# Five of nine attention tiles of each head pair transposed by the DMA as fp16 halves, instead of by TensorE in fp32

## The chip, the cores and the metric

The kernel runs on one core of a Trainium2 chip. TensorE does matmuls, and transposes as matmuls against an identity; VectorE (DVE), ScalarE (ACT) and GpSimd (POOL) do elementwise work; SyncE (SP) issues most DMAs, in the order in which they stand in its queue. The metric is the device time of one execution in microseconds, lower is better.

## The reference

Attention over 4 batches of 8 heads, 576 tokens, head size 64, with a threshold near the row's maximum; then a gated layer without an activation, and a second layer with one (all fp32):

```python
scores = scale * np.matmul(q, k.transpose(0, 1, 3, 2))
thresh = np.max(scores, axis=-1, keepdims=True) - tau
scores = np.where(scores >= thresh, scores, -1000000000.0)
scores = scores - np.max(scores, axis=-1, keepdims=True)
attn = np.exp(scores)
attn = attn / (np.sum(attn, axis=-1, keepdims=True) + 1e-09)
attn_out = np.matmul(attn, v)                    # (4, 8, 576, 64)
x = attn_out.transpose(0, 2, 1, 3).reshape(2304, 512)
h = (x @ w1) * (x @ w2) @ w3                     # w1, w2: 512x1024, w3: 1024x1024
x2 = h @ w_out                                   # 1024x512
h2 = x2 @ w_in                                   # 512x2048
y = np.where(h2 > 0, h2, np.exp(np.minimum(h2, 0)) - 1) @ w_out2
```

## The kernel before

**Pairs and tiles.** The 32 heads are 16 pairs, p = 0 to 15, and each pair has 9 tiles of 128 query rows (pos 0 to 8; the last holds the remaining 64 rows of both heads). So there are 144 tiles, i = 0 to 143. Pairs 0 to 3 go first, their first four tiles each, then their last five each; from tile 36 on (pair 4) each pair's nine tiles stand together. A pair's output is formed in two groups: n = 0 of the first four tiles (256 columns of queries a head), n = 1 of the last five (320 columns).

**One tile** is a chain: scores S on TensorE into a PSUM tile `s` (L317 for pairs 0 to 3, L329 later); the negated row maximum on DVE (`emit_max`, L338); a one-column threshold on POOL (`emit_tiny`, L342; for pairs 0 to 3 also a one-column bias, `emit_bias`, L346); the exponential on ACT (`emit_exp`, L351 and L353) into `e`; mask and row sum on DVE (`emit_mask`, L359); five transposes of 128 columns on TensorE back into the same `s` (`emit_X`, L370); and a copy on ACT into `pt`, P transposed (`emit_C`, L381 to L386). The ring of `s` has three tiles, and a slot is held from the scores to that copy. `e` has five buffers, `pt` two.

**After a group's tiles** come the reciprocal row sums on DVE (`emit_rr`, L394 and L395), turned on TensorE (L400), kept by ACT (L405), stored to DRAM by SP (`rd`, L412 and L414) and loaded back, spread over the partitions (`rb`, L422 to L428). P times V is ten fp32 matmuls (five blocks of 128 keys, two heads; each fp32 matmul stands as two instructions in the trace, so 20), the two heads writing different halves of the output partitions (`emit_PV`, L438). DVE multiplies by the reciprocals (`emit_xf`, L446), ACT rounds to fp32r (`emit_xh`, L450), and POOL forms the rest (`emit_xl`, L454): `x` is two fp32r halves.

**The gated layer** (`ab`, L475) of batches 0 to 2 runs in between as filler: 96 units of 12 matmuls (3 batches, 2 groups of columns, 8 weight blocks, 2 weights), which need `x` of a batch's four pairs. ACT keeps one factor (L483), DVE multiplies (L490), SP stores (`g_dr`, L494). The unit of weights `w12` is converted on the way (`conv_ops`, L205 to L230). `keep_busy` (L334) puts four matmuls on ones behind the scores of each of the first 18 tiles. The last batch's 32 units, and all that follows (`m` L743, `x` L883, `h` L916, `o` L945), come after the attention and stand in a fixed order.

**The order** of the attention stage is written by a planner (`Plan`): each operation has an engine, an assumed duration, the operations it follows, and a due time (in tiles); per engine, the operation that can start first goes next, the one due earliest where several can. The order so found is the program's order on each engine, and each engine runs its list in order. FA, FB and FC are the due times of the `ab` units (first batch's two column groups; later batches), C0 and CG those of the weight conversions.

Of the kernel before, what the change touches and what calls it, by code (L numbers as in the profile page):

```python
# [141 lines left out]
def attention_moe_moe2(  # L142
# [205 lines left out]
    def emit_exp(i):
# [3 lines left out]
        else:  # L352
            A.activation(et[i], sc[i][:, :, :HS], AF.Exp, bias=st[i][:, 0:1])  # L353
# [9 lines left out]

    def emit_X(i):
# [3 lines left out]
        for c in range(5):  # L368
            k = min(c * P, S - P)
            T.transpose(o[:, c * P:(c + 1) * P], e[:, k:k + P], ident)  # L370

    def emit_C(i):
        p, pos = SEQ[i]
        j, t = ORDER[pos]
        g = (p, int(pos >= 4))
        if g not in pt:
            pt[g] = ptp.tile([P, 5, 2, NW[1]], F32, tag="pt", name=f"pt{p}_{g[1]}")
        x = sc[i].rearrange("p a b -> p (a b)")[:, :5 * P].rearrange("p (c q) -> p c q", c=5)
        if p < NPL:
            c = (pos - 4 * g[1]) * P  # L380
            A.activation(pt[g].rearrange("p c j t -> p c (j t)")[:, :, c:c + P], x, AF.Copy)  # L381
        elif j == 2:
            A.activation(pt[g][:, :, :, 256:320], x.rearrange("p c (j q) -> p c j q", j=2), AF.Copy)
        else:
            c = (t % 2) * P
            A.activation(pt[g][:, :, j, c:c + P], x, AF.Copy)  # L386
# [43 lines left out]
    def emit_PV(p, n, c):  # L430
# [595 lines left out]
```

## Time and profile before

| | us |
|---|---|
| median of 3 runs (1088.04 to 1089.91) | 1089.19 |
| the profiled execution's own time | 1087.62 |
| its span, from first to last instruction | 1085.8 |
| attention stage, to the last batch's first `ab` matmul | 483.84 |
| the rest, to the end of the span | 602.0 |
| PE busy in the span | 1059.0 |
| DVE, ACT, POOL busy in the span | 554.6, 499.8, 346.5 |

The profiled execution lies 1.6 us under the median. An engine's busy time says how long any instruction of it was running; matmuls overlap each other, so a busy TensorE still may have waited a little. The chain of waits (followed back from the last instruction) says which engine's work each moment of the end time stands on. In the views below, `PEld` is TensorE's weight load, and "<-" in a name means "written from".

### The profile page before, as it was taken

What the parts mean: (1) busy time and instruction counts of PE and PEld (TensorE: products, weight loads), DVE (VectorE), ACT (ScalarE), POOL (GpSimd) and SP (SyncE); (2) the same over time, 40 slices, a digit from 0 to 9 for tenths busy, and PEclk for the clock granted to TensorE, in tenths of its full rate; (3) what the DMA queues carried; (4) which work ended last, traced back from release to release, by engine and by line L of the source; (5) the groups of instructions that cost most, each with busy time, mean ns of one, the idle gap of its engine ahead of it and who ended that gap; (6) DMA issues with size and microseconds to landing.
All of it is one profiled execution on the core that took longest, in us unless ns stands there. A gap on an engine that the chain in (4) does not pass through costs nothing.

```text
span 1085.8 us, 16950 instructions
## 1 busy us (share of the span) xinstructions
PE 1059.0 (98%) x6564; PEld 917.8 (85%) x6564; DVE 554.6 (51%) x998; ACT 499.8 (46%) x822; POOL 346.5 (32%) x418
## 2 busy tenths in 40 slices
PE   7989999999999999999999999999999999999998
PEld 4656777967888889889979999989999999999897
DVE  5887776266555555537483655863232333332322
ACT  3777666276556555534352556533232232322322
POOL 2657544234433332103340223232222222222221
PEclk9999999999999999999999999999999999999999
DMA  9233222213222220026634755300000000000000
GB/s 296 91 110 107 91 80 71 90 59 103 80 68 70 83 80 23 31 104 226 216 121 154 242 191 195 117 1 30 1 1 30 1 30 1 1 30 1 30 1 30
DMA packets 36461, 89.05 MB, mean 82 GB/s; under 512 B 4912, under 2 KB 23580, under 8 KB 31772
## 3 DMA queue, kind: packets, MB, share of 16 engines
q1 hardware_dynamic: 32268, 58.31, 16.9%
q10 hardware_dynamic: 4112, 29.66, 7.9%
q8 instruction: 51, 0.84, 0.3%
q14 instruction: 30, 0.25, 0.1%
HBM read 73.73 MB, written 14.23 MB: 81 GB/s over the span
## 4 chain that ended last, share of the span: by engine, by line
PE 90%; DVE 3%; DMA 2%; ACT 2%; issue 2%; SPq 1%; POOL 0%; DVEq 0%; ACTq 0%
PE h L916 18%; PE o L945 18%; PE ab L475 18%; PE x L883 9%; PE pv L438 8%; PE s L370 7%; PE s L329 5%; PE m L743 4%; PE s L317 2%; DVE e L359 1%; DMA rb<-rd 1%; DMA rqk<-in_qk 1%; DVE st L338 1%; DVE rr L394 1%; ACT e L353 0%
## 5 line engine op out<-in xcount | busy, mean ns | idle before, releaser
L475 PE MATMUL ab<-x,W 128*128 128x256 f32 (+1 forms) x1536 | 234.2, 301 | 1.2 <-DVE g L490 1.2
L475 PEld LDWEIGHTS ab<-x,W 128*128 128x128 f32 x1536 | 209.6, 188 | 12.1 <-issue 6.9
L945 PE MATMUL o<-WO,sl 128*128 128x512 f32 x864 | 215.7, 394 | 0.6 <-POOL sl L937 0.6
L916 PE MATMUL h<-sl,W 128*128 128x384 f32 x1152 | 215.7, 337 | 0.0
L916 PEld LDWEIGHTS h<-sl,W 128*128 128x128 f32 x1152 | 202.8, 188 | 8.3
L945 PEld LDWEIGHTS o<-WO,sl 128*128 128x128 f32 x864 | 161.1, 188 | 30.7 <-POOL sl L937 1.1
L937 POOL TENSOR_TENSOR sl<-th,sl 128x384 fp32r<-128x384 f32 x87 | 88.4, 1017 | 266.5 <-ACT sl L932 266.5
L359 DVE SCALAR_TENSOR_TENSOR e<-s,st,e 128x576 f32<-128x576 f32 x144 | 116.0, 813 | 64.1 <-ACT e L353 50.8
L925 DVE TENSOR_SCALAR th<-h 128x384 f32<-128x384 f32 x96 | 53.4, 556 | 182.3 <-PE h L916 182.3
L926 ACT ACTIVATE th<-th 128x384 f32<-128x384 f32 x96 | 50.4, 525 | 194.0 <-DVE th L925 194.0
L338 DVE TENSOR_REDUCE st<-s 128x1 f32<-128x576 f32 x144 | 107.3, 752 | 52.1 <-PE s L329 38.8
L370 PE MATMUL s<-ident,e 128*128 128x128 f32 x720 | 105.4, 279 | 5.9 <-DVE e L359 5.5
L370 PEld LDWEIGHTS s<-ident,e 128*128 128x128 f32 x720 | 80.1, 141 | 32.4 <-DVE e L359 17.9
L883 PE MATMUL x<-sl,M 128*128 128x384 f32 x576 | 100.9, 337 | 0.2 <-DVE sl L195 0.2
L883 PEld LDWEIGHTS x<-sl,M 128*128 128x128 f32 x576 | 99.7, 188 | 1.3 <-DVE sl L195 1.1
L342 POOL TENSOR_SCALAR st<-st,add 128x1 f32<-128x1 f32 x144 | 43.2, 300 | 172.5 <-DVE st L338 171.9
L438 PE MATMUL pv<-pt,vr 128*64 128x256 f32 (+1 forms) x640 | 94.2, 417 | 0.8 <-DVE g L490 0.8
L353 ACT ACTIVATE e<-s,st 128x576 f32<-128x576 f32 x108 | 78.5, 736 | 32.2 <-DVE st L338 31.7
L386 ACT ACTIVATE pt<-s 128x640 f32<-128x640 f32 x96 | 67.2, 702 | 54.3 <-PE s L370 54.1
L932 ACT ACTIVATE sl<-th 128x384 fp32r<-128x384 f32 x96 | 50.4, 525 | 77.7 <-PE o L945 47.9
L329 PE MATMUL s<-qk 128*128 128x288 f32 x480 | 83.8, 302 | 0.7 <-ACT pt L386 0.6
L930 DVE SCALAR_TENSOR_TENSOR th<-th,h 128x384 f32<-128x384 f32 x96 | 53.2, 554 | 58.6 <-ACT th L926 58.5
(76 smaller groups left out, 1047.4 us busy)
## 6 DMA issues: line engine op xcount, KB each, us to landing
rqk<-in_qk SPq DMA_DIRECT2D x24, 576.0 KB
raw_wo<-in_wo ACTq DMA_DIRECT2D x12, 1024.0 KB
th<-g_dr SPq DMA_DIRECT2D x48, 192.0 KB
raw_w<-in_w SPq DMA_DIRECT2D x8, 1024.0 KB
raw_w<-in_w3t ACTq DMA_DIRECT2D x8, 1024.0 KB
raw_win<-in_win ACTq DMA_DIRECT2D x8, 1024.0 KB
vr<-in_v SPq DMA_DIRECT2D x16, 320.0 KB
g_dr<-g SPq DMA_DIRECT2D x16, 320.0 KB
```

What stands on the lines that cost most here:

```text
L329: T.matmul(s[:, n, :HS], q, k[:, c:c + HS], start=(x == 0), stop=(x == len(ops) - 1))
L338: V.tensor_reduce(st[i][:, 0:1], sc[i][:, :, :HS], axis=AX.XY, op=ALU.max, negate=True)
L353: A.activation(et[i], sc[i][:, :, :HS], AF.Exp, bias=st[i][:, 0:1])
L359: V.scalar_tensor_tensor(et[i], sc[i][:, :, :HS], st[i][:, 1:2], et[i], op0=ALU.is_ge, op1=ALU.mult, accum_out=sm[p][:, pos:pos + 1],)
L370: T.transpose(o[:, c * P:(c + 1) * P], e[:, k:k + P], ident)
L386: A.activation(pt[g][:, :, j, c:c + P], x, AF.Copy)
L438: T.matmul(po_[p, n][j * D:(j + 1) * D, :w], vt[p][:, j, c * D:(c + 1) * D], x_, start=(c == 0), stop=(c == 4),)
L475: T.matmul(o[:, :w], wf[:, m, wx, kt, :], x[:, xx, :], start=(kt == 0 and k == 0), stop=(kt == NK - 1 and k == 2),)
L883: T.matmul(o[:, :TB], M[:, f, mx, e * P:(e + 1) * P], gh[j, f][:, gx, :], start=(k == 0), stop=(k == 23),)
L916: T.matmul(o[:, :TB], WI[f][:, wx, kt, :], xh[j, kt][:, xx, :], start=(k == 0), stop=(k == 3 * NK - 1),)
L937: (V if jobs else G).tensor_tensor(x[:, 1, :], thin[2 + f % 2], f32(x[:, 0, :]), op=ALU.subtract)
L945: T.matmul(po[j, t], gg[j, f][:, gx, t * P:(t + 1) * P], WO[f // 2][:, f % 2, wx, :], start=(f == 0 and k == 0), stop=(f == NF2 - 1 and k ...
```

## The change

The first four tiles of each pair, and all of pairs 0 and 2, stay as they are. The last five tiles of pairs 1, 3 and 4 to 15, 70 tiles, take another way from the mask on: ACT copies the masked `e` as fp16 (`emit_H`), POOL subtracts and writes the fp16 rest (`emit_L`, 512 and 64 columns), and SP issues a DMA transpose of the 128x1152 fp16 tile straight into `pt` (`emit_T`; two of 64 rows for a pair's last tile). The exponential's bias then carries a factor 2^14, which needs `emit_bias` on POOL for those tiles of pairs 4 to 15 too. V of those 14 groups is made fp16 halves as well, scaled by its mean (`v_sum` and `prep_v` on ACT, `v_mean` on TensorE, `v_scale` and `prep_vl` on DVE), and P times V of such a group is 28 fp16 matmuls of 320 columns (14 for each head). `emit_xl` moves from POOL to DVE for all 32 groups. `keep_busy` stands behind 9 tiles instead of 18, `e` has four buffers instead of five, the raw weights `w12` one instead of two. The planner's assumed durations and due times change, and transposes have a queue of their own in it ("DT", 2.7 us each and 2.5 more to land). The core of the diff:

```diff
-EB, PTB, VB = 5, 2, 4
-NKB = 18
+EB, HLB, PTB, VB, VHB = 4, 4, 2, 4, 2
+NKB = 9
...
-FA, FB, FC = (24.0, 44.0), (20.0, 36.0), (8.0, 36.0)
+FA, FB, FC = (22.0, 24.0), (46.0, 32.0), (6.0, 36.0)
...
+    def v_sum(p):
...
+        A.activation(v16[p][:, :, 0, :], vraw[p], AF.Abs, accum_out=vam[p])
+
+    def v_mean(p, i):
+        T.matmul(sc[i][:, 1, HS + P:HS + P + 1], spread, vam[p], start=True, stop=True)
...
+    def prep_v(p):
+        A.activation(v16[p][:, :, 0, :], vraw[p], AF.Copy, scale=vst[p][:, 1:2])
+
+    def prep_vl(p):
+        t = v16[p]
+        V.scalar_tensor_tensor(
+            t[:, :, 1, :], vraw[p], vst[p][:, 1:2], t[:, :, 0, :], op0=ALU.mult, op1=ALU.subtract
+        )
...
+    def of_dma(p, n):
+        return n == 1 and (p >= NPL or p % 2 == 1)
+
+    def by_dma(i):
+
+        return SEQ[i][1] >= 4 and of_dma(SEQ[i][0], 1)
...
+    def emit_H(i):
+        hl[i] = hlp.tile([P, 2 * S], F16, tag="hl", name=f"hl{i}")
+        A.activation(hl[i][:, :S], et[i].rearrange("p a b -> p (a b)"), AF.Copy)
+
+    def emit_L(i):
+        e, t = et[i].rearrange("p a b -> p (a b)"), hl[i]
+        G.tensor_tensor(t[:, S + 64:], e[:, :512], t[:, :512], op=ALU.subtract)
+        G.tensor_tensor(t[:, S:S + 64], e[:, 512:], t[:, 512:S], op=ALU.subtract)
...
+    def emit_T(i):
+        p, pos = SEQ[i]
+        if p >= NPL and ORDER[pos][0] == 2:
+            for j in range(2):
+                SP.dma_start_transpose(pt[p, 1][:, :, j, 256:320], hl[i][j * D:j * D + D, :])
+        else:
+            SP.dma_start_transpose(place(i), hl[i])
...
+    PVS = [(c, x, c) for c in range(5) for x in range(2)] + [(5 + c, 0, c) for c in range(4)]
+    PVC = [PVS[:3], PVS[3:6], PVS[6:9], PVS[9:12], PVS[12:]]
...
+        for c, x, vc in PVC[part]:
+            for j in range(2):
+                x_ = q[:, c, j, :w // D if p < NPL else w]
+                T.matmul(
+                    po_[p, n][j * D:(j + 1) * D, :w], v16[p][:, j, x, vc * D:(vc + 1) * D], x_,
+                    start=(c == 0 and x == 0), stop=(c == 8),
+                )
...
-        G.tensor_tensor(x[:, 1, :], xf[p, n][:, :NW[n]], f32(x[:, 0, :]), op=ALU.subtract)
+        V.tensor_tensor(x[:, 1, :], xf[p, n][:, :NW[n]], f32(x[:, 0, :]), op=ALU.subtract)
...
-        bi = op(call(emit_bias, i), [mx], "POOL", 0.15, i - 10) if plain else mx
+        bi = op(call(emit_bias, i), [mx], "POOL", 0.3, i - 10) if plain or by_dma(i) else mx
...
+        if by_dma(i):
+            hi = op(call(emit_H, i), [mk], "ACT", 0.66, i - 1)
+            rh = take("hl", HLB, hi)
+            lo = op(call(emit_L, i), [hi], "POOL", 1.6, i - 1)
+            re += [mk, hi, lo]
+            cs = [op(call(emit_T, i), [lo], "DT", 2.7, i - 1, 2.5)]
+            rh += [lo] + cs
```

**POOL, last five tiles of pair 14 (tiles 130 to 134).** In these names `st` is a tile's one-column statistics and `hl` its two fp16 halves; the number behind the name is the tile, and a last number tells buffers apart. Before:

```order
L454 TENSOR_TENSOR x13_1_4718<-xf13_1_4711,x13_1_4718 128x320
L342 TENSOR_SCALAR st131_4737<-st131_4737,add2_107 128x1
L342 TENSOR_SCALAR st132_4771<-st132_4771,add2_107 128x1
L342 TENSOR_SCALAR st133_4805<-st133_4805,add2_107 128x1
L342 TENSOR_SCALAR st134_4824<-st134_4824,add2_107 128x1
L454 TENSOR_TENSOR x14_0_4866<-xf14_0_4853,x14_0_4866 128x256
L342 TENSOR_SCALAR st135_4883<-st135_4883,add2_107 128x1
```

Now:

```order
L381 TENSOR_SCALAR st131_5074<-st131_5074 128x1
L377 TENSOR_SCALAR st131_5074<-st131_5074,add2_113 128x1
L381 TENSOR_SCALAR st132_5087<-st132_5087 128x1
L377 TENSOR_SCALAR st132_5087<-st132_5087,add2_113 128x1
L405 TENSOR_TENSOR hl131_5153<-e131_5123,hl131_5153 128x512
L406 TENSOR_TENSOR hl131_5153<-e131_5123,hl131_5153 128x64
L381 TENSOR_SCALAR st133_5160<-st133_5160 128x1
L377 TENSOR_SCALAR st133_5160<-st133_5160,add2_113 128x1
L381 TENSOR_SCALAR st134_5166<-st134_5166 128x1
L377 TENSOR_SCALAR st134_5166<-st134_5166,add2_113 128x1
L405 TENSOR_TENSOR hl132_5162<-e132_5133,hl132_5162 128x512
L406 TENSOR_TENSOR hl132_5162<-e132_5133,hl132_5162 128x64
```

Each of these tiles had one short instruction of POOL, and now has four: bias and threshold, which the exponential and the mask wait for, and the two subtractions, which stand in the same queue between those of later tiles. The subtractions of `x` are gone from POOL.

**SP, around the same tiles.** `rd` is the store of the reciprocal row sums of pair 14, groups 0 and 1, and `rb` their load; `g_dr` is a store of the gated layer. Before:

```order
L414 DMA rd14_0_4748<-rt14_0_4743 4x128
L425 DMA rb14_0_4778<-rd14_0_4748 128x1x256
L494 DMA g_dr_67<-g2_1_6_4734 128x2x320
L414 DMA rd14_1_4916<-rt14_1_4911 5x128
L425 DMA rb14_1_4952<-rd14_1_4916 128x1x256
L494 DMA g_dr_67<-g2_0_0_4902 128x2x256
L428 DMA rb14_1_4952<-rd14_1_4916 128x1x64
```

Now:

```order
L474 DMA rd14_0_5084<-rt14_0_5082 4x128
L434 DMA_TRANSPOSE pt14_1_5063<-hl130_5061 128x9x128
L485 DMA rb14_0_5125<-rd14_0_5084 128x1x256
L434 DMA_TRANSPOSE pt14_1_5063<-hl131_5153 128x9x128
L434 DMA_TRANSPOSE pt14_1_5063<-hl132_5162 128x9x128
L571 DMA g_dr_67<-g2_0_0_5142 128x2x256
L434 DMA_TRANSPOSE pt14_1_5063<-hl133_5202 128x9x128
L474 DMA rd14_1_5262<-rt14_1_5254 5x128
L432 DMA_TRANSPOSE pt14_1_5063<-hl134_5222 128x9x64 x2
L485 DMA rb14_1_5301<-rd14_1_5262 128x1x256
L488 DMA rb14_1_5301<-rd14_1_5262 128x1x64
```

Six transposes stand in SP's queue between the first store of pair 14 and the last load; a load of the reciprocals goes out only when the transpose ahead of it has been issued, and that one only when POOL has written its `hl`.

**TensorE, from the scores of tile 63 (pair 7).** `ab` names end in batch (attached), column group, weight block and weight. Before, with the many equal rows of units 0_1_0_1 to 0_1_7_0 left out:

```order
L329 MATMUL s64_2069<-qk10_1080 128x288 x4
L475 MATMUL ab0_0_7_1_2080<-x3_0_753,W7_1180 128x256 x3
L475 MATMUL ab0_1_0_0_2102<-x0_1_910,W0_274 128x320 x3
...
L475 MATMUL ab0_1_7_1_2345<-x2_1_1249,W7_1180 128x320 x3
L475 MATMUL ab0_1_7_1_2345<-x3_1_1415,W7_1180 128x320 x3
L370 MATMUL s62_2045<-ident_108,e62_2084 128x128 x5
L370 MATMUL s63_2064<-ident_108,e63_2094 128x128 x5
L370 MATMUL s64_2069<-ident_108,e64_2108 128x128 x5
```

Now:

```order
L364 MATMUL s64_2313<-qk10_1121 128x288 x4
L552 MATMUL ab0_1_4_1_2323<-x0_1_918,W4_743 128x320 x3
L552 MATMUL ab0_1_4_1_2323<-x1_1_1176,W4_743 128x320 x3
L552 MATMUL ab0_1_4_1_2323<-x2_1_1306,W4_743 128x320 x3
L552 MATMUL ab0_1_4_1_2323<-x3_1_1605,W4_743 128x320 x3
L364 MATMUL s65_2346<-qk11_1259 128x288 x4
L460 MATMUL s64_2313<-ident_114,rr6_1_2343 5x128
L552 MATMUL ab0_1_5_0_2357<-x0_1_918,W5_1022 128x320 x3
L552 MATMUL ab0_1_5_0_2357<-x1_1_1176,W5_1022 128x320 x3
L552 MATMUL ab0_1_5_0_2357<-x2_1_1306,W5_1022 128x320 x3
L442 MATMUL s63_2300<-ident_114,e63_2353 128x128 x4
```

Before, the second column group of the first batch, 16 units, stood as one run between the scores of tile 64 and the transposes of tiles 62 to 64, behind the last unit of the first group; now such units stand singly between tiles. Up to the scores of tile 36, 5.5 units of `ab` stand in TensorE's list before and 10.25 now; up to those of tile 72, 32 and 31. The P times V of the last five tiles of pairs 8 to 14 stands behind the scores of the fifth tile of the next pair, before and now; that of pairs 3 to 5 stood behind the third or fourth, and now behind the sixth or seventh.

## Rows read from the trace of the kernel before

**Rows 1.** The page: TensorE's busy time and instructions; its granted clock in 40 slices.

```profile
PE 1059.0 (98%) x6564; PEld 917.8 (85%) x6564; DVE 554.6 (51%) x998; ACT 499.8 (46%) x822; POOL 346.5 (32%) x418
...
PEclk9999999999999999999999999999999999999999
```

**Rows 2.** Chain of waits, its longest pieces in order of time: start, length, what.

```profile
63.56 6.89 DMA rb<-rd
...
189.59 29.58 PE ab L475 x204
...
470.85 4.26 PE ab L475 x36
475.11 2.84 PE pv L438 x20
...
483.84 51.15 PE ab L475 x384
```

**Rows 3.** Chain of waits, shares by line, in 0:119, 119:190, 119:484 and 264:484.

```profile
by line: PE s L317 20.6%; PE s L370 13.7%; PE pv L438 12.5%; DMA rqk<-in_qk 9.3%; PE ab L475 5.9%; DMA rb<-rd 5.8%; issue 5.3%; SPq L259 3.9%; DVE e L359 3.5%; PE k L334 3.3%; DVE rr L394 3.3%; ACT pt L381 2.8%; DVE st L338 1.5%; ACT e L351
...
by line: PE pv L438 23.4%; PE s L329 22.5%; PE s L370 16.0%; PE ab L475 9.8%; DVE e L359 9.2%; issue 4.6%; DVE st L338 4.1%; DVE rr L394 3.6%; ACT e L353 1.9%; PE s L400 1.7%; ACT qk L279 1.6%; DVE g L490 0.8%; ACT x L450 0.4%; DVE rr L395 
...
by line: PE ab L475 36.5%; PE pv L438 18.3%; PE s L329 16.1%; PE s L370 16.1%; DVE e L359 2.7%; issue 2.3%; ACT e L353 1.5%; DVE st L338 1.4%; DMA rb<-rd 1.2%; PE s L400 0.9%; DVE rr L394 0.7%; ACT qk L279 0.6%; ACT pt L386 0.6%; DVE g L490
...
by line: PE ab L475 44.1%; PE pv L438 18.8%; PE s L370 17.3%; PE s L329 16.2%; DVE e L359 0.8%; PE s L400 0.7%; DVE st L338 0.7%; ACT e L353 0.6%; DVE g L490 0.4%; issue 0.3%; ACT rt L405 0.2%; DVEq L490 0.0%; DVEq L359 0.0%
```

**Rows 4.** Stretches: length; busy (instructions) of PE, PEld, DVE, ACT, POOL; clock, DMA, GB/s.

```profile
119.00:190.00 71.00, 67.98 (x509) 53.45 (x508) 49.91 (x107) 47.99 (x77) 30.46 (x51) 1.00 0.26 81
190.00:219.00 29.00, 29.00 (x201) 29.00 (x200) 7.07 (x18) 6.85 (x14) 7.95 (x10) 1.00 0.25 84
264.00:484.00 220.00, 218.70 (x1638) 187.51 (x1637) 119.81 (x259) 116.75 (x195) 65.18 (x108) 1.00 0.21 64
119.00:484.00 365.00, 356.51 (x2638) 300.73 (x2637) 207.26 (x448) 202.70 (x335) 123.09 (x197) 1.00 0.23 70
```

**Rows 5.** Groups by form, DVE, 119:190: shapes, count; busy us, mean ns; idle before.

```profile
L359 DVE SCALAR_TENSOR_TENSOR e<-s,st,e 128x576 f32<-128x576 f32 x27 | 21.4, 810 | 1.1 <-ACT e L353 0.7
...
L394 DVE TENSOR_SCALAR rr<-sm 128x5 f32<-128x5 f32 x3 | 2.8, 923 | 0.0
```

**Rows 6.** Groups by form, TensorE, 264:484.

```profile
L370 PE MATMUL s<-ident,e 128*128 128x128 f32 x310 | 45.4, 277 | 0.1
```

**Rows 7.** Timeline of TensorE, 290:297: start, length, line, operation, shapes, count.

```profile
291.18 1.92 PE L475 MATMUL ab<-x,W 128*128 128x320 f32 x12
292.93 0.70 PE L329 MATMUL s<-qk 128*128 128x288 f32 x4
```

**Rows 8.** Groups by form, the whole span.

```profile
L386 ACT ACTIVATE pt<-s 128x640 f32<-128x640 f32 x96 | 67.2, 702 | 54.3 <-PE s L370 54.1
...
L334 PE MATMUL k<-spread 128*128 128x128 f32 x72 | 10.5, 290 | 0.0
...
L342 POOL TENSOR_SCALAR st<-st,add 128x1 f32<-128x1 f32 x144 | 43.2, 300 | 172.5 <-DVE st L338 171.9
...
L230 POOL TENSOR_TENSOR W<-w_win,W 128x1024 fp32r<-128x1024 f32 x8 | 19.3, 2418 | 69.4 <-ACT W L227 69.4
...
L454 POOL TENSOR_TENSOR x<-xf,x 128x320 fp32r<-128x320 f32 x16 | 14.0, 876 | 39.5 <-ACT x L450 39.5
...
L454 POOL TENSOR_TENSOR x<-xf,x 128x256 fp32r<-128x256 f32 x16 | 11.8, 736 | 17.6 <-ACT x L450 17.1
...
L446 DVE TENSOR_TENSOR xf<-pv,rb 128x320 f32<-128x320 f32 x16 | 7.8, 489 | 5.8 <-DMA rb<-rd 2.3 <-PE pv L438 1.7 <-PE s L370 1.5
```

**Rows 9.** The line of DVE's reciprocal sums: count, min/median/max ns, first and last start.

```profile
L394 DVE TENSOR_SCALAR rr<-sm x32: 161/191/1972, 23.1 to 467.6; 128x4 f32<-128x4 f32 x16, 128x5 f32<-128x5 f32 x16
```

**Rows 10.** The DMA queue's own waits: engine, line, what for; total, times, longest.

```profile
SPq L425 <- DMA rd<-rt: 26.6, 23, 2.8
```

**Rows 11.** The page, DMA queue of SP: packets, MB, share of 16 engines' span.

```profile
q1 hardware_dynamic: 32268, 58.31, 16.9%
```

More of the change, by code (lines that the diff above doesn't have):

```diff
@@ L368, in emit_X @@
         for c in range(5):
-            k = min(c * P, S - P)
-            T.transpose(o[:, c * P:(c + 1) * P], e[:, k:k + P], ident)
+            k = min(P, S - c * P)
+            T.transpose(o[:k, c * P:(c + 1) * P], e[:, c * P:c * P + k], ident)
     def emit_C(i):
[L373 to L386, printed above, removed]
+        x = sc[i].rearrange("p a b -> p (a b)")[:, :5 * P].rearrange("p (c q) -> p c q", q=P)
+        A.activation(place(i), x, AF.Copy)
     rrs, rts, rdr, rbc, po_, xf, xT = {}, {}, {}, {}, {}, {}, {}
@@ L496, in store_g @@
         )
-    V.memset(spread, 1.0)
+    V.memset(spread, 1.0 / VSCALE)
     for p in range(NPL):
@@ L567, in attention_moe_moe2 @@
     for p in range(NPAIR):
-        lv = op(call(load_v, p), (), "SP", 0.1, AT[p, 0] - 3, 4.0)
-        VV[p] = [lv]
-        ring["v", p] = take("vr", VB, lv)
+        t0 = AT[p, 0]
+        lv = op(call(load_v, p), (), "SP", 0.1, t0 - 6, 4.0)
+        rv = ring["vr", p] = take("vr", VB, lv)
+        VV[p, 0] = VV[p, 1] = [lv]
+        if not of_dma(p, 1):
+            continue
+        t0 = AT[p, 4] - 1
+        vm = op(call(v_sum, p), [lv], "ACT", 0.8, t0 - 3)
+        am = take("am", 2, vm)
+        i = t0 + 3
+        vs = op(call(v_mean, p, i), [vm, S_[i]], "PE", 0.15, t0 - 1)
+        am.append(vs)
+        ve = op(call(v_scale, p, i), [vs], "DVE", 0.3, t0 - 1)
+        ring["s", i] += [vs, ve]
+        rt = take("vst", 5, ve)
+        vh = op(call(prep_v, p), [ve], "ACT", 0.8, t0)
+        vl = op(call(prep_vl, p), [vh], "DVE", 1.17, t0)
+        rv += [vm, vh, vl]
+        rt += [vh, vl]
+        ring["vst", p] = rt
+        ring["v16", p] = take("v16", VHB, vm)
+        VV[p, 1] = [vh, vl]
     for p in range(NPL, NPAIR):
@@ L620, in attention_moe_moe2 @@
         rb.append(xo)
-        ring["v", p].append(pv)
+        if of_dma(p, n):
+            ring["vst", p].append(xo)
+            ring["v16", p].append(pv)
+        else:
+            ring["vr", p].append(pv)
         ring["pt", p, n].append(pv)
         xh = op(call(emit_xh, p, n), [xo], "ACT", (0.36, 0.42)[n], q)
-        xl = op(call(emit_xl, p, n), [xh], "POOL", (0.73, 0.91)[n], q)
+        xl = op(call(emit_xl, p, n), [xh], "DVE", (0.4, 0.46)[n], q)
         rx += [xh, xl]
```

110 lines of the change are left out of this document (77 added, 33 removed).

## The prediction

> **What bounds the kernel now.** I read the page first: TensorE is busy for 1059 us of the span of 1085.8, in 6564 matmuls, and its granted clock stands at 9 or more tenths in every slice [rows 1]. Such a row does not say that matmuls set the end at every moment, so the chain of waits comes next. From 483.84 us on it is the last batch's `ab` and then the later layers, which the change does not touch [rows 2]; those 602 us I leave as they are. In front of that lie three stretches. From 0 to 119 us (36 tiles, pairs 0 to 3) TensorE's lines make only 56% of the chain (20.6, 13.7, 12.5, 5.9, 3.3), so some 52 us there are waits. From 119 to 190 they make 73.4%, and from 264 to 484 they make 97.1%; over the whole of 119 to 484 they make 87.9% of 365 us, that is 321 us of matmuls and 44 us of waits [rows 3]. In between, at 189.6 us, stands one run of 29.58 us of `ab` alone [rows 2], in which DVE and ACT are busy for 7 of 29 us [rows 4]. Over 119 to 484 DVE is busy for 207 us, ACT for 203 and POOL for 123 [rows 4]. So from 119 us on TensorE's amount of work is the bound, and before that the tile chain.
>
> **What the change removes from TensorE.** In the stretch from 264 to 484 the transposes hold 17.3% of 220 us [rows 3], and there are 310 of them, 62 tiles' worth [rows 6]: 0.614 us a tile. Pairs 4 to 15 lose 60 of these groups: 36.8 us. Over the longer stretch the same division gives 16.1% of 365 for 109 tiles, 0.54 us, which is the lower bound (32 us).
>
> P times V of a last-five group takes 2.84 us now [rows 2]. The new one has 14 pairs of fp16 matmuls of 320 columns. A unit of 12 single-pass matmuls of 320 columns starts at 291.18 and the next work at 292.93 [rows 7]: 0.146 us each. That the two heads' matmuls run side by side, in different output partitions, is seen from the fp32 ones: 20 instructions in 2.84 us are 0.142 us for 320 columns, 0.44 ns a column, while fp32 matmuls on the full width need 10.5 us for 72 of 128 columns [rows 8], 1.14 ns a column. So I take 14 x 0.146 = 2.05 us, and gain 0.79 x 12 = 9.5 us. Were the fp16 pairs to run one after another, a group would take 28 x 0.146 = 4.09 us, 1.25 more than today; the sum would be 24.5 us worse. Nothing in the trace shows an fp16 matmul; I take the pair, since the nearest row, the fp32 one, has it.
>
> `v_mean` adds 12 matmuls of one column. Their bound is the 0.146 us of a full-width fp32 instruction: +1.8 us.
>
> The units of `ab` that now stand before tile 36 (10.25 instead of 5.5) take 4.75 x 1.42 us (36 matmuls in 4.26 us, [rows 2]) = 6.7 us out of the later stretch and put them among the 52 us of waits of the first one. The run of 29.58 us is dissolved by the same move; this changes no amount of TensorE's work, but the other engines work beside it.
>
> In the first stretch 10 transposing groups (6.1 us), two P times V (1.6 us) and nine `keep_busy` (36 x 0.146 = 5.3 us) go and 6.7 us come. I count that stretch at nothing, since the chain there waits for 52 us anyway; its bounds are 6 us either way. The cover of the removed `keep_busy` is the granted clock, which stays up now [rows 1]; if it fell to 1.2 GHz in the waits of that stretch, its 67 us of matmuls would partly double, so this price could reach 10 us.
>
> TensorE's work from 119 to 484 becomes 321 - 36.8 - 9.5 + 1.8 - 6.7 = 270 us.
>
> **What it adds elsewhere.** ACT: the fp16 copy (576 columns) stands in for a copy of 640 at 0.702 us [rows 8], I take them as equal; the two passes over V at that same price are 12 x 1.4 = 17 us on an engine with 160 us free. POOL: by the rows of 256 and 1024 columns (0.736 and 2.418 us [rows 8]) a column costs 2.2 ns, and 512 plus 64 columns come to 1.6 us a tile; 60 tiles are 97 us, 60 biases at the 0.300 us of the threshold [rows 8] are 18, and the moved `x` rests save 12 x 1.61 = 19. POOL goes from 123 to 219 us. That is for fp32; with an fp16 operand it may be half or double, and double would be 316 us. DVE: 24 `x` rests at about 0.49 us [rows 8], 12 of `prep_vl` at about 0.9 and the small `v_scale`: 12 x 2.2 = 26 us, so 207 becomes 233. All stay under TensorE's 270.
>
> A DMA transpose moves 128 x 1152 fp16, 0.29 MB. No row shows one. The lower bound is its bytes: SP's queue moved 58.31 MB in 16.9% of the span [rows 11], 0.318 MB a us, so 0.93 us. The upper is the longest `rb` load on the chain, 6.89 us [rows 2]. A store of the row sums holds back the load behind it for 26.6/23 = 1.2 us [rows 10], so I take some 2.5 us. It matters only above a limit: five transposes a pair, at a pair's 27 us, may take 5.4 us each. The landing is covered too: P times V of pairs 8 to 14 still stands behind the scores of the next pair's fifth tile, five tiles or about 15 us on, and of those the mask (0.81 us [rows 5]), two passes of its like for maximum and exponential, the fp16 copy and the rest take about 3 x 0.81 + 0.70 + 1.6 = 4.7 us. In the list of SP the loads of the reciprocals now stand behind transposes, which wait for POOL; a late `rb` holds `emit_xf`, and behind it all of DVE.
>
> One wait grows for certain. The reciprocal sums on DVE, 0.161 us at the shortest, took up to 1.972 [rows 9], and 0.923 in the mean of three where POOL works long [rows 5]. The longer ones start under a long POOL instruction. The 36 new two-input operations of DVE and 24 such sums will meet POOL at work 219 of some 320 us: 0.67 x half of 1.3 us is 0.44 us each for the 36, and a third of a POOL instruction's half more for the sums, 16 + 5 = 21 us of DVE. DVE has slack, so I put 10 on the path.
>
> The Trainium skill ("SBUF — State Buffer", section "Who interferes with whom") says that a DVE instruction with two inputs in SBUF, or a tensor_scalar in a fast mode, and a GpSimd instruction that reads SBUF exclude each other for the whole instruction. The trace agrees in the reciprocal sums, 0.161 against 1.972 us; for the two-input form it would give the 21 us above, and without it only the 5 us of the sums.
>
> **The sum.** 270 us of matmuls, the 44 us of waits, 10 more: 324 for 365, a gain of 41. The profiled execution's 1087.6 become 1046.2, and with the 1.6 us by which the median lies above it 1048; I say 1047. The pace this asks of the tile chain, 324/109 = 2.97 us a tile, is slower than what it ran at from 119 to 190, 71/27 = 2.63 us a tile [rows 4, 5], with three score tiles then held until the copy; the 70 tiles now free theirs after the mask.
>
> **The rivals.**
> *More is gained.* The waits shrink with the work: at the share of today, 12.1%, 270 us give 307 in all, and with 6 us of the first stretch the time is 1025. For it speaks the freed score ring; against it that DVE's slack falls.
> *Part is eaten.* The fp16 pairs run in turn (24.5 us), or DVE's 21 us and late `rb` loads all count: 1060 to 1085.
> *Slower: the chain, not TensorE.* The share of waits of 119 to 190, 26.6% [rows 3], over all the new work: 270/0.734 = 368 for 365; with DVE's 21 us in full 389, and 1113. It decides from a share of 26%. POOL at double price ends there too. For it: DVE's share rises to that of that stretch (50 of 71 us [rows 4]). Against it: that stretch had little `ab` to fill in, 15 - 5.5 units for three pairs, where now each pair has some seven.
> *Slower: the transposes are the bound.* 70 of them from about 75 us on, with 25 us behind the last: 75 + 70 t + 25 against 484, so from t = 5.5 us. At 6.89 us it is 582, and the time 1187. For it: nothing known of t. Against it: bytes alone need 0.93.
> The Trainium skill ("VectorE: DVE Perf Modes", "The three transpose paths") has 1309 ns for one 128x128 block through the DMA; nine in turn would be 11.8 us, and the estimate from that 1528 us. Another page ("Advanced Engine Details and Errata", "X-Bar Transpose (TRN2)") has transposes as fast as other DMAs, which is the lower bound. No row shows either; the first alone I give 2 in 100, within the chance of this rival.
>
> **How the numbers follow.** The forecast (1030 to 1062) gets 0.60, more gained 0.14, part eaten 0.13, no change 0.02, the chain 0.06, the transposes 0.05. The three runs before lie within 0.2%, which is about what a measurement can tell here; so faster 0.87, same 0.02, slower 0.11. The range runs from 1022 (just under the case of more gained) to 1085 (all of part eaten), and leaves out the slower cases and a little below.
>
> **What would show it.** Right: the last batch's `ab` starts near 442 us instead of 483.84; 74 groups of transposes at about 0.61 us; the new P times V near 2.05 us; TensorE over 80% of the chain from tile 36 on; no long run of `ab`. Wrong: matmuls of P times V that wait for a DMA, a P times V near 4 us, POOL's subtractions well over 1.6 us, DVE's two-input operations far over 0.5 us, a granted clock below full in the first 60 us. The forecast fails most surely if transposes take over 5.5 us each, or if the waits pass a quarter of the attention stage.

## The result, and the profile after

| | before | after |
|---|---|---|
| median us (4 runs each) | 1088.65 | 1072.68 (1071.12 to 1075.20) |
| ratio, 95% interval | | 0.9854 [0.9832, 0.9876] |
| profiled execution | 1087.62 | 1072.06 |
| span | 1085.8 | 1070.3 |
| last batch's `ab` starts | 483.84 | 468.14 |
| the rest, to the end | 602.0 | 602.2 |

Faster by 1.5%, 16 us where 41 were forecast. The whole of it lies in the attention stage: the last batch's `ab` starts 15.7 us earlier, and what follows takes as long as before. The page after, to be read against [rows 1] and [rows 11] (busy time, share and instructions; then tenths of the clock in 40 slices; then the DMA queue's packets, MB and share of 16 engines):

```profile
PE 1016.3 (95%) x6318; PEld 888.7 (83%) x6318; DVE 584.4 (55%) x1072; ACT 515.0 (48%) x864; POOL 440.1 (41%) x586
...
PEclk9999999998999999999999999999999999999999
...
q1 hardware_dynamic: 115532, 78.97, 30.1%
```

TensorE lost 43 us of busy time, POOL gained 94 and VectorE 30, and SP's queue holds the DMA engines for 322 us (30.1% of 1070.3) where it held them for 183. The end of the attention stage, from the chain of waits (start, length, what), against [rows 2]:

```profile
447.32 5.07 DMA rb<-rd
459.48 4.41 DMA pt<-hl
463.93 3.58 PE pv L510 x27
468.14 51.15 PE ab L552 x384
```

Before, `ab` and P times V stood on that path back to back; now a load of reciprocals, a transpose and a P times V at the slower clock come just ahead of the last run (granted clock 0.50 from 464 to 466 us). The trace follows this chain back only to 379.6 us; of the 88 us from there to the last `ab`, TensorE's lines hold 49%, where over 80% was named as a sign of being right:

```profile
by line: PE ab L552 19.5%; PE pv L510 11.4%; DMA pt<-hl 8.2%; PE s L364 7.9%; PE s L442 7.5%; DVE e L394 6.4%; DMA rb<-rd 5.8%; issue 4.1%; POOL hl L405 4.0%; DVE st L373 3.1%; PE pv L502 2.8%; DVE x L531 2.7%; DVE rr L454 2.6%; DMA rd<-rt
```

Where the time came from is seen best in stretches that end at the same tile, the scores of tile 36 (first instruction of that line: 118.8 before, 129.0 after) and those of tile 90 (290.7 and 290.5). Busy time by engine, clock and DMA share, before:

```profile
0.00:119.00 119.00, 105.68 (x761) 68.37 (x762) 86.45 (x164) 76.22 (x108) 65.52 (x107) 0.99 0.45 144
...
290.00:483.84 193.84, 192.54 (x1449) 165.23 (x1447) 104.94 (x227) 101.69 (x171) 56.68 (x94) 1.00 0.20 61
sum 483.84, PE 462.03 PEld 368.94 DVE 293.71 ACT 278.92 POOL 188.61; mean PE 115.51 PEld 92.23 DVE 73.43 ACT 69.73 POOL 47.15
```

and after:

```profile
0.00:129.00 129.00, 108.74 (x748) 68.93 (x749) 88.47 (x175) 79.84 (x118) 66.99 (x113) 0.95 0.55 151
129.00:257.00 128.00, 108.77 (x821) 92.84 (x819) 96.79 (x208) 87.26 (x148) 94.52 (x155) 0.97 0.74 138
257.00:290.00 33.00, 33.00 (x246) 29.60 (x246) 19.81 (x44) 19.71 (x35) 17.91 (x29) 1.00 0.58 136
290.00:468.14 178.14, 168.97 (x1343) 148.43 (x1341) 118.76 (x259) 106.67 (x187) 102.29 (x176) 0.99 0.52 122
sum 468.14, PE 419.47 PEld 339.80 DVE 323.83 ACT 293.50 POOL 281.71; mean PE 104.87 PEld 84.95 DVE 80.96 ACT 73.37 POOL 70.43
```

In the sums, TensorE is busy 42.6 us less (462.03 to 419.47), but idle 48.7 us where it was idle 21.8. The difference, 15.7 us, is the gain. By tile 90, with 40 of the 70 tiles done the new way, nothing was gained. By the starts of the row maxima, 13 us were lost up to tile 36 (133, before 120), 22 won back by tile 72 (227, before 236), where the lone run of `ab` stood, and 9 lost again by tile 81 (258 both). The 30 tiles after tile 90 gave 16.

Who made VectorE wait from tile 36 on (us in total, times, longest), before:

```profile
DVE e L359 <- ACT e L353: 50.8, 46, 1.9
DVE g L490 <- PE ab L475: 49.4, 25, 5.4
DVE st L338 <- PE s L329: 38.8, 41, 2.6
DVE xf L446 <- DMA rb<-rd: 5.4, 3, 2.8
```

and after:

```profile
DVE e L394 <- ACT e L388: 24.5, 27, 1.9
DVE xf L521 <- PE pv L510: 13.0, 4, 6.1
DVE g L567 <- PE ab L552: 12.1, 10, 3.0
DVE xf L521 <- DMA rb<-rd: 10.6, 5, 3.1
DVE e L394 <- POOL st L377: 7.7, 11, 1.7
DVE xf L519 <- DMA rb<-rd: 6.9, 5, 2.5
DVE st L373 <- PE s L364: 6.8, 10, 1.6
```

Before, VectorE waited for TensorE's scores and `ab`, 88 us of them: TensorE was the bound. Now that is 19 us. The largest wait, for ScalarE's exponentials, is half of what it was (24.5 of 50.8), and new waits are for DMA loads (17.5), for POOL, and for P times V, whose own wait was for the DMA (the page's group of L510 has 10.0 us idle, 7.8 of it for `pt`).

One such place, from the timeline (start, length, engine, line, operation, idle before):

```profile
229.28 2.09 PE L510 MATMUL pv<-pt,v 128*64 128x320 f16 x28
...
245.39 3.98 SPq L432 DMA_TRANSPOSE pt<-hl  x2
...
251.10 0.30 PE L510 MATMUL pv<-pt,v 128*64 128x320 f16 x1 [2.44 <-DMA pt<-hl]
251.60 3.59 PE L510 MATMUL pv<-pt,v 128*64 128x320 f16 x27 [0.20 <-DMA pt<-hl]
255.23 0.55 DVE L521 SCALAR_TENSOR_TENSOR xf<-pv,vst,rb 128x320 f32<-128x320 f32 x1 [3.97 <-PE pv L510]
```

The ninth tile of a pair is transposed in two halves, the last thing ahead of P times V. SP issues them from 245.39 to 249.37; TensorE waits for them 2.44 us, its clock falls (granted 0.50 from 252 to 255 us; an earlier fall, from 242 to 245, was over by then), so the same 28 matmuls that took 2.09 us at 229 take 3.9, and VectorE, with every mask behind `xf` in its list, waits 3.97.

### The profile page after: what moved, and what is told of

Its sections match the earlier page's. It is cut to its first block, busy times and chain, and to the rows that moved or that the text cites. A ratio compares the mean times of both kernels' runs of the same rounds, so it can differ in the third digit from the quotient of the medians.

```text
span 1070.3 us, 17023 instructions
## 1 busy us (share of the span) xinstructions
PE 1016.3 (95%) x6318; PEld 888.7 (83%) x6318; DVE 584.4 (55%) x1072; ACT 515.0 (48%) x864; POOL 440.1 (41%) x586
## 3 DMA queue, kind: packets, MB, share of 16 engines
q1 hardware_dynamic: 115532, 78.97, 30.1%
## 4 chain that ended last, share of the span: by engine, by line
PE 59%; DMA 2%; DVE 2%; POOL 1%; ACT 1%; issue 1%; SPq 0%; POOLq 0%; DVEq 0%; ACTq 0%
PE h L1031 19%; PE o L1060 19%; PE x L998 9%; PE ab L552 6%; PE m L858 4%; PE pv L510 1%; DMA pt<-hl 1%; PE s L364 1%; PE s L442 1%; DVE e L394 1%; DMA rb<-rd 0%; DMA th<-g_dr 0%; POOL hl L405 0%; DVE st L373 0%; PE pv L502 0%
## 5 line engine op out<-in xcount | busy, mean ns | idle before, releaser
L394 DVE SCALAR_TENSOR_TENSOR e<-s,st,e 128x576 f32<-128x576 f32 x144 | 115.3, 813 | 40.0 <-ACT e L388 24.5
L405 POOL TENSOR_TENSOR hl<-e,hl 128x512 f16<-128x512 f32 x70 | 82.7, 1181 | 32.8 <-ACT hl L401 32.4
L364 PEld LDWEIGHTS s<-qk 128*128 128x128 f32 x480 | 69.1, 190 | 16.9 <-issue 6.4
L446 ACT ACTIVATE pt<-s 128x640 f32<-128x640 f32 x74 | 51.6, 702 | 41.0 <-PE s L442 36.8
L442 PE MATMUL s<-ident,e 128*128 128x128 f32 (+1 forms) x370 | 56.0, 285 | 9.1 <-DVE e L394 9.0
L235 POOL TENSOR_TENSOR WO<-w_wo,WO 128x1024 fp32r<-128x1024 f32 x12 | 29.9, 2488 | 79.7 <-ACT WO L232 77.3
```

What stands on the lines that cost most here:

```text
L364: T.matmul(s[:, n, :HS], q, k[:, c:c + HS], start=(x == 0), stop=(x == len(ops) - 1))
L394: V.scalar_tensor_tensor(et[i], sc[i][:, :, :HS], st[i][:, 1:2], et[i], op0=ALU.is_ge, op1=ALU.mult, accum_out=sm[p][:, pos:pos + 1],)
L405: G.tensor_tensor(t[:, S + 64:], e[:, :512], t[:, :512], op=ALU.subtract)
L442: T.transpose(o[:k, c * P:(c + 1) * P], e[:, c * P:c * P + k], ident)
```

## The experiments

Four theories of the missing 25 us. **A**: POOL's list (biases, thresholds and subtractions in one queue) holds the tile's chain. **B**: the DMA brings P and the reciprocals late. **C**: VectorE's own load. **D**: the clock, since `keep_busy` went. Beside these, the order and the buffers. "Tile 36" is the start of its row maximum on VectorE, the 37th of that group (120 us before, 133 after). Such a time is of one profiled execution; in e2, which edits only the tiles from 36 on, it is 138, so a few us there tell little. Where no other kernel is named, the edit is to the changed kernel (1072.68 us). Where an operation changes its engine or a ring its size, the planner's entry for it changes too. Ratios are to the kernel before.

**e1, plain copies.**

```diff
-SP.dma_start_transpose(place(i), hl[i])
+SP.dma_start(place(i), hl[i].rearrange("p (c t) -> p c t", c=TPP))
```

> The changed kernel, but each DMA transpose is a plain DMA copy of the same bytes to the same place (P then reaches P times V untransposed: this part of the computation is left out). The accounts so far: against the kernel before, 36 us of the attention stage were to be gained from tile 36 on and 10 us were lost ahead of it; TensorE stands idle 48 us before the last batch's ab, where it stood 22. Theory A (POOL's queue: biases, thresholds and subtractions in one list hold the tile's chain): nothing changes, 1070 to 1075 us. Theory B (the DMA engines, 0.80 busy from 129 to 202 us, bring P and the reciprocals late): 1056 to 1065 us, with the PE waits for pt and DVE waits for rb gone, if the copies are lighter for the DMA engines than the transposes; if the DMA share of 129 to 202 us stays near 0.8, this run says nothing of B.

Measured 1065.29 us, 0.9789 [0.9741, 0.9837]: 7.4 less, its interval just touching that of the changed kernel. From 129 to 202 us the last-but-one column, the DMA share, is 0.80 in the changed kernel

```profile
129.00:202.00 73.00, 65.30 (x513) 56.22 (x513) 58.11 (x124) 51.61 (x89) 55.50 (x92) 1.00 0.80 141
```

and here

```profile
129.00:202.00 73.00, 68.22 (x536) 58.82 (x535) 59.69 (x126) 54.54 (x93) 59.05 (x95) 1.00 0.59 149
```

so the copies are lighter, and SP issues one in 0.63 us (median) instead of 1.31. VectorE's waits for `rb` from tile 36 on fall from 17.5 us to 8.8. B has a part, at the small end of its range; whether by the DMA engines' load or by SP's time to issue isn't told apart.

**e2, no bias on POOL from tile 36 on.**

```diff
-bi = op(call(emit_bias, i), [mx], "POOL", 0.3, i - 10) if plain or by_dma(i) else mx
+bi = op(call(emit_bias, i), [mx], "POOL", 0.3, i - 10) if plain else mx
```

> The changed kernel without POOL's bias for the tiles from 36 on (P is not scaled by 2^14 there, so its fp16 halves keep fewer bits; 60 POOL instructions of 0.2 to 0.3 us go, and the exponential waits for the maximum alone). Theory A: ACT waited some 25 us for biases in all, 8.5 us of it from tile 36 on, and the maximum-to-exponential hop gets about 0.4 us shorter per tile; 1062 to 1069 us. Theory B (DMA) and theory C (VectorE's own load): 1070 to 1075 us.

Measured 1067.69 us, 0.9793 [0.9775, 0.9811]: 5.0 less, as A said.

**e3, the subtraction on VectorE** (`G.` becomes `V.` in `emit_L`).

> The changed kernel with the subtraction that makes P's low fp16 half on VectorE instead of POOL (512 and 64 columns, an estimated 0.8 us a tile there, from the 0.54 us of a two-input subtraction of 320 columns with POOL at rest, instead of 1.56 us on POOL). POOL falls by some 109 us, VectorE rises by some 55. Theory A (POOL's list): 1060 to 1069 us. Theory C (VectorE is the fuller engine up to tile 81, 58 of 73 us from 129 to 202, and everything that it gets more is late): 1077 to 1095 us. Theory B: near 1072.

Measured 1099.38 us, 1.0088 [1.0072, 1.0104]: 26.7 more. The two pieces take 0.68 and 0.22 us there (medians):

```profile
L405 DVE TENSOR_TENSOR hl<-e,hl x70: 673/683/1935, 87.1 to 479.9; 128x512 f16<-128x512 f32 x70
L406 DVE TENSOR_TENSOR hl<-e,hl x70: 208/218/1446, 87.7 to 480.5; 128x64 f16<-128x64 f32 x70
```

VectorE's busy time rises by 57 us (641.4 from 584.4), POOL's falls by 97, and nearly half of VectorE's rise is on the path. So VectorE has little slack (C), and the subtraction stands rightly on POOL.

**e4, 18 `keep_busy` again** (`NKB = 18`).

> The changed kernel with the 18 keep_busy groups of before instead of 9. Theory D (the clock: the granted clock is 0.87 to 0.96 in the slices from 40 to 120 us, where it stood at 1.00): the mean clock rises from 0.989 to at least 0.994 and the time falls to 1065 to 1069 us. Theories A, B and C: 36 more matmuls of 0.13 us in a stretch that waits, 1071 to 1076 us.

Measured 1075.03 us, 0.9862 [0.9832, 0.9893], mean clock 0.981: no gain, and D's remedy doesn't hold the clock.

**e5, pairs 1 and 3 back on TensorE.**

```diff
-return n == 1 and (p >= NPL or p % 2 == 1)
+return n == 1 and p >= NPL
```

> The changed kernel, but the last five tiles of pairs 1 and 3 (10 of the first 36 tiles) stay fp32 on TensorE as before; all later pairs go through the DMA. The first 36 tiles took 10 to 14 us longer after the change. If the new steps of a tile (fp16 copy, subtraction, transpose, the two passes over V) make that, tile 36 comes at 120 to 124 us instead of 130 to 133 and the time is 1062 to 1067 us. If the order does (the units of ab ahead, one buffer instead of two for the loads of w12, the place of the first loads), tile 36 stays near 131 us and the time is 1071 to 1077 us.

Measured 1073.28 us, 0.9852 [0.9825, 0.9879]; tile 36 at 132 us. The new steps don't make the lateness of the first 36 tiles, and ten removed tiles there gain nothing.

**e6, the due times of before** (FA, FB, FC).

> The changed kernel with the due times of ab of before (24 over 44, 20 over 36, 8 over 36). If the units of ab that were drawn ahead of tile 36 make its lateness, tile 36 comes at 120 to 125 us; what of it stays at the last batch's ab depends on whether the run of ab alone comes back near tile 63 to 72: 1064 to 1070 us if it doesn't, 1072 to 1080 if it does. If the new steps make it, tile 36 stays near 131 us and the time is 1072 to 1085 us.

Measured 1090.59 us, 0.9998 [0.9972, 1.0024], above both ranges; tile 36 at 133 us. Without the new due times the change gains nothing. The chain of waits shows why:

```profile
162.59 20.07 PE ab L552 x138
```

The run of `ab` alone is back, at tile 45 to 63, and in 160 to 180 us VectorE works 7.0 us of 20 and ScalarE 5.2. Tile 63 comes 23 us later than in the changed kernel (228, 205), and the last batch's `ab` 19 us later (487.4, 468.1): the rest has no slack in which to catch up.

**e7, the rest of `x` on POOL** (`V.` becomes `G.` in `emit_xl`).

> The changed kernel with the rest of x (32 subtractions of 256 or 320 columns) back on POOL. VectorE loses 32 x 0.55 to 0.82, some 21 us, POOL gets an estimated 26 us. e3 gave VectorE 40 us of busy time more up to 468 us and the time rose by 27 us. Theory C (VectorE's share of the chain sets the pace): two thirds of 21 us, so 1056 to 1066 us. Theory A (POOL's list): 1074 to 1082 us. If both count: near 1070.

Measured 1070.07 us, 0.9838 [0.9798, 0.9878]: not told from the changed kernel. Neither C's two thirds of 21 us nor A's loss shows; the time is where both together were expected, so the two may cancel.

**e8, the reciprocals' stores and loads from ScalarE** (`SP.` becomes `A.` in `store_r` and `load_r`).

> The changed kernel with the stores and loads of the reciprocals (rd, rb) issued by ScalarE instead of SP, so that they stand behind no transpose in SP's list. After the change SP waited 3.3 us a time for the store of rd where it waited 1.2 us, and VectorE's xf waited 10.6 us for rb. Theory B in the form that SP's list holds rb back: 1062 to 1068 us. If it is the DMA engines' own load (0.80 busy from 129 to 202 us), or POOL or VectorE: 1071 to 1080 us, the more since ScalarE pays some 0.5 us an issue (76 issues).

Measured 1069.45 us, 0.9818 [0.9792, 0.9843]: 3.2 less by the medians, between the two ranges, the intervals overlap. That the reciprocals stand behind transposes in SP's list is at most a small part.

**e9, the kernel before with one buffer for `w12`.**

```diff
-name=f"raw_{key[0]}{key[1]}", bufs=2)
+name=f"raw_{key[0]}{key[1]}", bufs=1 if key[0] == "w12" else 2)
```

> The kernel before, with one buffer instead of two for the loads of w12, and nothing else of the change. In e4 to e6 tile 36's maximum came at 132 to 137 us (120 before) whether or not the first pairs went through the DMA and whichever due times stood. If the single buffer makes that, tile 36 comes at 127 to 133 us here and the time is 1092 to 1102 us. If not, tile 36 stays at 119 to 122 us and the time at 1087 to 1091 us.

Measured 1094.50 us, 1.0047 [1.0027, 1.0066], tile 36 at 127 us. One line of the change, which the prediction passed over, costs 5 us.

**e10, the kernel before with the new due times.**

> The kernel before, with the new due times of ab (22 over 24, 46 over 32, 6 over 36) and nothing else of the change. e6 was as slow as the kernel before without them. If the new order carries the gain by itself: 1068 to 1076 us. If it only lets the removed work count (TensorE of before was idle for 8 us from tile 36 on, so that an order can give no more there): 1080 to 1092 us.

Measured 1086.83 us, 0.9968 [0.9955, 0.9980]. Tile 36 comes at 130 us here too; the 10 us are won back by tile 72 (235, before 236). The new order draws work ahead, and gives about 3 us alone.

**e11, e2 + e7 + e8 together.**

> The changed kernel with e2, e7 and e8 together: no bias on POOL from tile 36 on (P unscaled there, so its fp16 halves keep fewer bits), the rest of x on POOL, the reciprocals on ScalarE's queue. If the three waits are different ones, their gains of 5.0, 2.6 and 3.2 us add: 1059 to 1064 us. If they are one wait seen from three sides (the chain of a tile), 1065 to 1069 us.

Measured 1065.42 us, 0.9774 [0.9732, 0.9816]: 7.3 less by the medians. The interval, some 1060 to 1070 us, holds the 10.8 of the sum too, so three waits and one wait seen from three sides are not told apart.

**e12, only pairs 8 to 15 by the DMA.**

> The changed kernel, but only pairs 8 to 15 (from tile 72 on, 40 of the 70 tiles) go through the DMA; the 30 others stay fp32 on TensorE. If a removed transpose and the cheaper P times V pay wherever they stand, 0.61 + 0.16 us a tile come back 30 times: 1085 to 1097 us. If they pay only where TensorE is the bound, and the tile chain sets the pace ahead of tile 72: 1066 to 1076 us.

Measured 1078.61 us, 0.9901 [0.9870, 0.9933]: 5.9 us for 30 tiles put back by the medians, 0.2 a tile (the intervals just touch). Neither range: early tiles pay about a quarter of the 0.77 us that a tile takes off TensorE.

**e13 and e14, smaller rings, with two and one buffers for `w12`.** Both have `EB` 3 for 4 and `HLB` 2 for 4; e13 also the two buffers of before.

> The changed kernel with two buffers for the loads of w12 again; to make room, 3 buffers instead of 4 for P and 2 instead of 4 for its fp16 halves. Compared with e14, which has the same small rings and one buffer. If the single buffer holds back the first 36 tiles here as it did in e9: tile 36 comes 5 to 9 us earlier than in e14 and the time is 4 to 7 us lower. If the loss there has another cause: within 2 us of e14.

> The control of e13: the changed kernel with 3 buffers instead of 4 for P and 2 instead of 4 for its fp16 halves, and one buffer for w12 as in the changed kernel. If the steps of a tile (copy, subtraction, transpose) hold a buffer no longer than some three tiles, nothing changes: 1070 to 1076 us. If the rings themselves hold the chain: 1078 to 1095 us.

e14 measured 1099.96 us, 1.0096 [1.0060, 1.0132], e13 1088.27 us, 0.9988 [0.9975, 1.0002]. The small rings cost 27 us, the second buffer is worth 12 beside them. But tile 36 comes at 132 and 133 us, and the two part from there to tile 45 (159 and 169): so the single buffer was a cost here too, and not the cause of the first 36 tiles' lateness.

**e15, e11 with the plain copies of e1.**

> e11 (three reliefs) with the plain DMA copies of e1 in place of the transposes (P reaches P times V untransposed: this part of the computation is left out). If the DMA's load is a cost apart from POOL and VectorE, the gains add, 1065.4 - 7.4: 1055 to 1060 us. If the copies only shortened the same chain: 1062 to 1067 us.

Measured 1054.40 us, 0.9687 [0.9656, 0.9718]: 11.0 under e11, the intervals clear of each other. What the transposes cost against copies (B) is apart from the part of POOL and VectorE, and together they are 18 us.

**e16, whole-tile transposes twice.**

```diff
-SP.dma_start_transpose(place(i), hl[i])
+for _ in range(2):
+    SP.dma_start_transpose(place(i), hl[i])
```

> The changed kernel with every whole-tile DMA transpose (58 of the 82 instructions) issued twice to the same place, so that SP issues 58 x 1.3 us more and the DMA engines carry some 2 us a tile more (141 us of 16 engines for 70 tiles now, by the queue's share). If the transposes are hidden behind a tile's pace of 2.7 us: 1071 to 1077 us. If the DMA's load sets the pace ahead of tile 81 (0.80 busy from 129 to 202 us): 1085 to 1110 us.

Measured 1234.23 us, 1.1347 [1.1308, 1.1386], far above both ranges. The edit did more than double a load. Both transposes write the same place, and SP issued the second only when the first had landed, as SP's own waits (whole span) say:

```profile
SPq L435 <- DMA pt<-hl: 156.5, 58, 6.3
```

SP stands still for 156.5 us, 2.7 us a time, and the kernel is 161.5 us slower. All else in SP's list stands behind these waits. The other engines' waits from 129 to 560 us:

```profile
PE pv L511 <- DMA pt<-hl: 56.1, 14, 14.5
...
DVE xf L522 <- DMA rb<-rd: 46.6, 5, 14.1
...
POOL rqk L271 <- DMA rqk<-in_qk: 98.6, 11, 17.8
```

P, the reciprocals and the next pair's Q and K all come late, though the DMA engines are busy for only 0.62 to 0.67 of 129 to 428 us. So this run can't tell what the transposes' load costs: the time that it lost is about that of the waits in SP's list. From tile 36 to 143 it takes 453 us (154 to 607) for 107 tiles, 38 us a pair, in which nine whole transposes pass (four twice, the ninth tile once): 4.2 us each, these waits included, is an upper bound. How fast transposes pass without them wasn't measured.

**e17, e11 with the fifth buffer of P back** (`EB` 5; 7 for 8 of the first `x` ring, one for two turned reciprocals).

> e11 (three reliefs) with 5 buffers for P again instead of 4; to make room, 7 instead of 8 for x of the first four tiles and one instead of two for the turned reciprocals. If the rings still hold the chain at 4 (e14, with 3 and 2, was 27 us slower than with 4 and 4): 1056 to 1062 us. If four are enough: 1063 to 1070 us, as e11's 1065.4.

Measured 1072.08 us, 0.9853 [0.9823, 0.9883], above both ranges and 6.7 more than e11. The buffers it borrowed cost more than the fifth of P gives.

**e18, the kernel before with one buffer for `w12` and four for P.**

> The kernel before with one buffer instead of two for w12 and 4 instead of 5 for P: the room that the change takes, and nothing else of it. e9 measured the first of these at 1094.5 us, 4.8 above before. If the fifth buffer of P is spare in the kernel before, where P waits for TensorE's transposes alone: 1092 to 1097 us. If it isn't: 1098 to 1110 us.

Measured 1096.57 us, 1.0066 [1.0053, 1.0079]: the room that the change takes costs 7 us here, some 5 of it the `w12` buffer by e9; the intervals of the two runs overlap, so the fifth buffer of P is not shown to cost anything.

## Why the prediction was right and wrong

**The work that goes from TensorE was right.** I went through TensorE's instructions ahead of the last `ab` and counted each from its start, or the end of the one before it, to its end, by line. Transposes: 91.3 to 49.4 us for 350 fewer, 0.60 us a tile (0.614 forecast). P times V: 88.2 to 80.5, 0.55 a group against 0.79; at full clock a new group takes the 2.09 us shown above, against 2.05 forecast, so the heads' fp16 matmuls do run side by side. `keep_busy`: -4.6. `v_mean`: +2.0 (1.8 forecast). Together 52 us; by the forecast's prices the whole stage was to lose 58.

**Ten of them came back as slower matmuls.** Scores took 114.8 us instead of 107.8 and `ab` 159.7 instead of 157.3, for the same instructions. The granted clock was 0.83 to 0.96 in six stretches of 20 us (40 to 120, 240 to 260, 460 to 480), a mix of the levels 2.4 and 1.2 GHz and some 24 us at the lower one. The prediction bounded this by 10 us, but for the missing `keep_busy` and the first stretch alone, and put it at nothing in the sum; e4 shows that those matmuls are not the remedy. In the place shown above, a wait of 2.44 us stands ahead of the slow matmuls; that waits cause all of the falls wasn't tried.

**The step that failed is "the 44 us of waits, 10 more", and with it the first stretch, which I "count at nothing".** In the terms of the sum, the 25 us that are missing stand in three places. The first 36 tiles took 10 us more (118.8 to 129.0). From there on TensorE's work fell by 46 us (356.5 [rows 4] to 310.7, the sum of the three rows after 129) instead of 51, with some of the matmuls slower. And its idle time there grew by 20 us, from 8.5 [rows 4] to 28.4, where 10 were forecast; in the whole stage it grew by 27 (21.8 to 48.7). Behind the idle time stand costs that I had put at nothing, or nearly. The runs show two of them in the changed kernel; the third, the room, is carried over from the kernel before.

*The transposes, "it matters only above a limit".* The limit was 5.4 us each, and it wasn't reached: they take at most 4.2 even with the waits of e16, so five take at most 21 of the 26.6 us of a pair from tile 36 to 143 (133 to 450 us). I took all below the limit as hidden. But with plain copies in their place 7.4 us come back (e1), with the reliefs there 11.0 (e15). What of a transpose costs this, its load on the DMA engines, SP's time to issue it or its landing, stays open. Seen in the trace is that P comes late for P times V in the place above, the reciprocals for `xf`, and behind `xf` VectorE's masks. That P times V of pairs 8 to 14 is covered was right (none of the seven waits for `pt`); those of three others wait, as the one above, whose last transposes are issued just ahead of it. By the Trainium skill ("VectorE: DVE Perf Modes", "The three transpose paths") nine blocks of 1309 ns in turn would be an estimated 11.8 us a tile. In e16 a whole tile had landed some 4 us after SP began to issue it (1.3 to issue, 2.7 of waiting), which denies it. The Trainium skill ("Advanced Engine Details and Errata", "X-Bar Transpose (TRN2)") has transposes as fast as other DMAs. That is nearer, but not met either: 322 us of SP's queue against 287 with copies (27.0% of 1063.8) are 0.5 us a tile more.

*POOL and VectorE in the tile's chain.* The price of each instruction was right: subtraction 1.18 + 0.38 = 1.56 us (1.6 forecast), VectorE +30 us busy (26 without exclusion). The wait that was to grow "for certain", 21 us of VectorE with 10 on the path, hardly did: the reciprocal sums took 16.6 us in all before and 15.1 after, and only the `x` rests of 256 columns stand out, with 0.82 us in the mean and 0.39 at the shortest. The place of the instructions was wrong. The biases were counted as 18 us of an engine with room; they stand between maximum and exponential, and without them 5.0 us come back (e2). e3 shows how little room VectorE has: 57 us more work, 27 us more time. All three reliefs are worth 7.3 (e11).

*The room.* The one-buffer load of `w12` and the fifth buffer of P are two numbers of the diff that the prediction did not price; in the kernel before they cost 7 us (e18). What they cost in the changed kernel alone no run shows.

Reliefs and copies together gave 18.3 us (e15). With the 7 of the room that is 25, the size of the miss, but the agreement proves nothing: the room was measured in the other kernel (in e13 against e14 the same buffer was worth 12), the reliefs undo a part that the forecast had priced, the `x` rests on VectorE, and e15 has TensorE still idle for 37.5 us ahead of the last `ab` (454.0 us, 416.5 of them busy). What holds the rest stays open.

**"I count that stretch at nothing"**, with bounds of 6 us, was wrong by 10. By the row maxima tile 36 came 13 us late, in the kernel before with the new order alone 10 (e10), and with the one buffer alone 7 (e9); with old due times (e6), without the first pairs' transposes (e5) or with two buffers (e13) it stayed at 132 or 133. So no single part taken away removes it; which make it stays open. In e10, where the same order draws work ahead, it was won back by tile 72; the forecast had credited that work (6.7 us) to the later stretch and charged nothing here.

**"The run of `ab` is dissolved; this changes no amount of TensorE's work"** was right, and missed what it is worth. In the kernel before, where TensorE was the bound, the due times gave 3 us. In the changed kernel they give 18 (e6), for there a run of `ab` stops three other engines that are nearly as full as TensorE (in 129 to 257 us VectorE works 97, ScalarE 87 and POOL 95 of 128 us, TensorE 109). The gain of the change is that of both parts together; neither alone has more than 3 us of it.

**Of the rivals**, "part is eaten" (1060 to 1085) is what happened, in part through late `rb` loads as it said, not through P times V in turn and hardly through VectorE's 21 us. "The chain, not TensorE" describes the stage up to tile 81, and by the chain's 49% its end too. "The transposes are the bound" was not met: they stayed under 4.2 us, where it began at 5.5.

e11 is the fastest of the kernels here that do all the work, 7.3 us under the changed kernel, with fewer bits in P.

## What to carry to other kernels

Work below its limit is not free: the transposes stayed under the time that a pair gave them, and still cost 7 to 11 us against plain copies. A list that is run in order passes every wait on to all that stands behind it: with 156 us of new waits in SP's list e16 was 161 us slower. So before a doubled load is read as the load's price, ask what the second copy waits for. Price the buffers that an edit takes, too, by taking them from the kernel before. And where work goes from the bounding engine, ask which engines are then level with it: there an order that lets one run alone, worth little before, decides.

## What the runs showed of the hardware

A DMA transpose of 128x1152 fp16 holds SP for 1.31 us (median), a plain copy of the same bytes for 0.63 (e1). The transpose has landed 2.7 us after SP has issued it, in the mean of 58 (e16). fp16 matmuls of 320 columns for two heads run side by side, 28 in 2.09 us at a granted clock of 1.00. A subtraction of 512 fp32 columns into fp16 takes 0.68 us on VectorE (median, e3) and 1.18 on POOL (mean).
